# Linear attention ahead of a mixture of experts: row-tiled projections, column-tiled sums, and gates moved to the expert steps

## The chip, the core and the metric

The kernel runs on one core of one Trainium2 chip. The metric is device time in microseconds (us) of one execution; before the change it was 753.89 us (median of 3 runs, 752.79 to 762.47). The engines that matter are TensorE (PE in the profile; its weight loads are listed apart as PEld), VectorE (DVE), ScalarE (ACT), GpSimd (POOL) and the sequencer that issues most transfers (SP).

## The reference

Eight sequences of 576 tokens go through attention with random features (8 heads of 64 values, 128 features); each token is then sent to one of 8 experts.

```python
def phi(x):
    proj = np.einsum('bhsd,md->bhsm', x, omega)
    h = proj - np.sum(x * x, axis=-1, keepdims=True) / 2.0
    h = h - np.max(h, axis=-1, keepdims=True)
    return np.exp(h) / np.sqrt(m)
q_p, k_p = phi(q * scale), phi(k * scale)
kv = np.einsum('bhsm,bhsd->bhmd', k_p, v)
z = np.sum(k_p, axis=2)
x = einsum(q_p, kv) / (einsum(q_p, z) + 1e-06)          # (4608, 512) after a transpose
...
logits = normalized(x) @ normalized(expert_emb).T / tau
expert_idx = np.argmax(logits, axis=1)
gate_w = softmax(logits) at expert_idx
out[token] = gate_w * (relu(x @ w1[e]) @ w2[e])          # 512 -> 1024 -> 512
```

Inputs and outputs are float32. The term with the square of x cancels in the subtraction of the maximum, so the kernel leaves it out.

## The kernel before

**Attention.** The tokens are 36 tiles of 128 rows (`NTILE`), nine tiles for a pair of sequences (`TPS`), so that the fifth tile of nine (u = 4) has 64 rows of each. A loop over i does the key side of tile i and, `LAG` = 6 iterations later, the query side of tile iq = i - 6. All work of an iteration comes in two halves of four heads each:

- `halves` (L303) splits the loaded keys or queries into a high and a low part on POOL (L309, L310), and `feats` (L313) makes the projection from three products of 256 columns for each pair of heads (L319: high by high, high by low, low by high). In such a product the transposed features of omega are laid out block-diagonally for two heads of 64 values, so all 128 rows of the array are used. DVE takes the maximum of each head (L324), ACT the exponential, one head at a time (L327).
- `kvmm` (L330) adds features times values (with a column of ones) into PSUM, one product for each head, 128 features wide and 65 columns long (L341); after a sequence `kvfin`, `kvfin1`, `kvfin2` (L351, L356, L366) copy the sums, turn them and multiply them with the expert embedding, so that the logits come out as eight more columns.
- `qtr` (L377) turns the query features with four transposes for a half (L381) and copies them out on ACT (L385) or DVE (L387).
- `num` (L391) multiplies them with the sums (L405; the numerator, the denominator and the logits, 73 columns for each head). In a tile with u = 4 the product is written in two parts of 64 tokens, each with its own sums. DVE then divides (L408 to L414), and ACT sums the squares of the tile (L420).
- Every three tiles (`G`) `route`, `route1` and `gates` find the expert of each token, its place, and its gate: the norm by `root` (a Newton iteration of small DVE operations, L119 to L130), the softmax by one small exponential (L444). POOL then scatters the rows of the three tiles with the gate and the token's number behind them to DRAM (L471).

PE and POOL follow the order in which the code is written (a manual schedule); a scheduler orders DVE and ACT. The transposes of `qtr` are written between the products of `kvmm`.

**Tail of attention.** Once the fullest expert is known (`pick_first`, after tile 17), its weights are loaded and split, and `first_steps` (here called the fill, in pieces of three products) computes two tiles of 128 of its tokens between the last iterations and in the planning that follows: DVE works out a table of 38 expert steps (L662 to L734), which PE turns (L738) and SP reads (`tabi`, L739).

**Expert steps.** From t = 2 on each step takes 128 tokens of one expert: 24 products of 512 columns for the first layer (`pa`) and 24 for the second (`po`), float32 in three products of split halves (L251). The turned activations go through transposing DMAs (L815), with ACT and DVE copies around them (L808, L809, L827, L829, L841 to L847). Each step also splits one quarter of the next expert's weights (L216, L217), multiplies the result by the gate (`scaled`, L258) and scatters it (L261). Here all engines follow the code.

## Time and profile before

| | |
|---|---|
| median of 3 runs | 753.89 us |
| profiled execution | 756.55 us, its span 754.9 us |
| six first tiles, keys only | to 33.8 us |
| 30 tiles, keys and queries | 33.8 to 266.4 us |
| last six query tiles, fill, planning | 266.4 to 335.0 us |
| expert steps | from 335.0 us on |
| PE, DVE, ACT, POOL busy | 96%, 73%, 51%, 55% |

The rows below that begin with two times are from the timeline: start and duration in us, engine, line, operation, output and inputs, the number of instructions that the row joins, and in brackets the idle time before it with what ended it. Durations overlap, since a following instruction begins while the one before it is finishing; what an instruction costs in a busy queue is therefore the distance between two starts. A row of the windows gives a stretch, its length, the busy time of PE, PEld, DVE, ACT and POOL with their instructions, then the granted TensorE clock, the share of the DMA engines and GB/s.

### The profile page before, as it was taken

The numbers are of one execution on the slowest core, as the hardware profiler recorded it, in microseconds if no ns is written. First come the engines' busy times: TensorE is split into PE (matmuls) and PEld (weight loads), VectorE is DVE, ScalarE is ACT, GpSimd is POOL, SyncE is SP. The second block draws the span as 40 slices with busy tenths as digits, with TensorE's granted clock in tenths as the row PEclk, the third lists the DMA queues.
The fourth block names the chain that finished last, engine by engine and source line by source line (L and its number), as shares of the span: only waits on it lengthen the run. The fifth ranks groups of instructions, "written<-read, shape, count | busy, mean of one in ns | idle before, by whom it ended". The sixth has DMA issues, their size and how long they took to land. (4 is left out here: it accounts for less than half of the span.)

```text
span 754.9 us, 15226 instructions
## 1 busy us (share of the span) xinstructions
PE 722.3 (96%) x4475; PEld 628.6 (83%) x4476; DVE 549.5 (73%) x1288; ACT 381.8 (51%) x974; POOL 416.7 (55%) x385
## 2 busy tenths in 40 slices
PE   6899999999998988989999999999999999999994
PEld 6899999999888978877788888888888888888883
DVE  6468888998899888836579766686676676676661
ACT  4577777776786765425224334434434334434320
POOL 5754665677648843244456546456546546545544
PEclk9899999999999999999999999999999999999998
DMA  6543344454584421179587877977877887887730
GB/s 200 154 142 87 114 154 142 127 169 144 160 273 123 160 70 58 57 245 289 149 224 221 233 189 210 233 189 213 228 188 209 224 199 211 220 210 202 199 106 38
DMA packets 142353, 131.38 MB, mean 174 GB/s; under 512 B 106745, under 2 KB 106873, under 8 KB 142275
## 3 DMA queue, kind: packets, MB, share of 16 engines
q1 hardware_dynamic: 135954, 110.15, 53.2%
q0 software_dynamic: 6320, 20.23, 7.0%
q8 instruction: 43, 0.70, 0.4%
q14 instruction: 36, 0.29, 0.1%
HBM read 83.65 MB, written 21.80 MB: 140 GB/s over the span
## 5 line engine op out<-in xcount | busy, mean ns | idle before, releaser
L217 POOL TENSOR_TENSOR w1l<-raww,w1h 128x1024 f32 x34 | 89.0, 2616 | 158.0 <-DVE w1h L216 158.0
L251 PE MATMUL po<-w2h,hl 128*128 (+1 forms) x288 | 114.3, 397 | 0.2 <-DVE hl L847 0.2
L251 PE MATMUL po<-w2h,hh 128*128 (+1 forms) x288 | 114.4, 397 | 0.0
L251 PE MATMUL po<-w2l,hh 128*128 (+1 forms) x288 | 114.2, 396 | 0.0
L808 ACT ACTIVATE pl<-pa 128x512 uint16<-128x512 uint16 x68 | 40.4, 596 | 141.2 <-PE pa L251 130.9
L251 PE MATMUL pa<-w1h,xh 128*128 (+1 forms) x280 | 111.4, 398 | 0.0
L251 PE MATMUL pa<-w1l,xh 128*128 (+1 forms) x280 | 111.0, 396 | 0.0
L251 PE MATMUL pa<-w1h,xl 128*128 (+1 forms) x280 | 111.0, 396 | 0.0
L327 ACT ACTIVATE ftk<-pjk,nmk 128x128 f32<-128x128 f32 x288 | 82.8, 376 | 52.9 <-DVE nmk L324 27.9
L809 DVE COPY pl<-pa 128x512 uint16<-128x512 uint16 x68 | 46.8, 690 | 68.4 <-ACT pl L808 68.3
L327 ACT ACTIVATE ftq<-pjq,nmq 128x128 f32<-128x128 f32 x288 | 84.5, 396 | 13.0 <-DVE nmq L324 7.6
L827 DVE COPY wd<-t 128x1024 uint16<-128x1024 uint16 x68 | 86.0, 1269 | 0.4 <-DMA t<-pl 0.4
L217 POOL TENSOR_TENSOR w2l<-raww,w2h 128x1024 f32 x34 | 82.2, 2418 | 6.7 <-DVE w2h L216 5.3
L341 PE MATMUL kva<-vt,ftk 128*128 128x65 f32 x576 | 85.4, 260 | 0.0
L341 PEld LDWEIGHTS kva<-vt,ftk 128*128 128x128 f32 x576 | 82.4, 197 | 0.0
L381 PE MATMUL tr<-ident,ftq 128*128 128x128 f32 x288 | 75.0, 281 | 1.9 <-ACT qp L385 1.7
L405 PE MATMUL pn<-kvs,qp 128*128 128x73 f32 (+1 forms) x640 | 71.7, 264 | 3.1 <-DVE xr L414 3.1
L843 ACT ACTIVATE hh<-wd 128x1024 fp32r<-128x1024 f32 x34 | 36.1, 1061 | 72.0 <-DVE wd L827 72.0
L405 PEld LDWEIGHTS pn<-kvs,qp 128*128 128x128 f32 (+1 forms) x640 | 67.7, 182 | 5.0 <-DVE xr L414 2.3
L319 PE MATMUL pjk<-w1l,w1h 128*128 128x256 f32 x288 | 63.2, 312 | 5.5 <-DVE w1h L309 5.5
L251 PEld LDWEIGHTS po<-w2h,hl 128*128 128x128 f32 x288 | 54.2, 188 | 13.8 <-DVE hl L847 0.7
L251 PEld LDWEIGHTS po<-w2h,hh 128*128 128x128 f32 x288 | 54.3, 188 | 13.3 <-POOL w2l L217 0.3
(237 smaller groups left out, 1610.9 us busy)
## 6 DMA issues: line engine op xcount, KB each, us to landing
raww<-w1q SPq DMA_DIRECT2D x38, 512.0 KB
raww<-w2q SPq DMA_DIRECT2D x38, 512.0 KB
vt<-v SPq DMA_DIRECT2D x36, 260.0 KB
kt<-kT SPq DMA_DIRECT2D x36, 256.0 KB
qt<-qT SPq DMA_DIRECT2D x36, 256.0 KB
xgp<-xs SPq DMA_DIRECT2D x20, 257.0 KB
xg<-xs SPq DMA_DIRECT2D x18, 257.0 KB
rf<-w1q SPq DMA_DIRECT2D x4, 512.0 KB
```

The source lines that it names most:

```text
L217: il = nc.gpsimd.tensor_tensor(at(l, dp), raw, at(h, dp).bitcast(F32), op=ALU.subtract)
L251: done.append(nc.tensor.matmul(dst, x[:, c * P : (c + 1) * P], ws.rearrange("p o f -> p (o f)"), start=(begin and i == 0 and k == 0), stop ...
L319: nc.tensor.matmul(pj[:, 2 * a : 2 * a + 2, :].rearrange("p a m -> p (a m)"), x[:, 2 * half + a, :], o, start=n == 0, stop=n == 2,)
L327: nc.scalar.activation(ft[:, h, :], pj[:, h, :], AF.Exp, bias=nm[:, h : h + 1])
L341: nc.tensor.matmul(acc[:, h, :], ft[:, h, :], vt[:, 4 * half + h, :], start=begin and h == 0, stop=u == 4 + 4 * b and h == 3,)
L381: nc.tensor.transpose(tr[:, h * P : (h + 1) * P], ft[:, h, :], ident)
L405: nc.tensor.matmul(pn[lo:hi, h, :], qp[:, h, lo:hi], kvs[sb, b][:, 4 * half + h, :], start=True, stop=True)
L808: nc.scalar.activation(planes[1][:, o : o + 512], halved(src)[:, :, 1], AF.Copy)
L809: nc.vector.tensor_copy(planes[0][:, o : o + 512], halved(src)[:, :, 0])
L827: nc.vector.tensor_copy(to, src)
L843: nc.scalar.activation(hh, wd[:, 0:F], AF.Relu)
```

## The change

In attention the loads of 64 values for a head stay in plain float32, with no split. A half is now made of the heads of one parity: `a` = 0 has its values in rows 0 to 63 of the array and `a` = 1 in rows 64 to 127, and `proj` writes the products of two such halves (one of the keys, one of the queries) alternately, into different banks. `kvmm`, `num` and the logits of the sums write each product in two parts of 64 output rows. The outputs of `num` for the two parities are two fixed tiles `nu[0]` and `nu[1]`; the transposes of a = 0 and the turns of the sums use them too, while the last query transposes (when no keys are left) take banks of their own. The whole loop is written out for DVE and ACT as well. `root` may run on POOL and does so for the embedding. The norm and the softmax leave attention: the row in DRAM carries the eight shifted logits in place of the gate, and the expert steps sum the squares, take a root, and make the gates for three steps at once. The fill runs in two to four pieces an iteration.

```diff
-PAY = DM + 2
+PAY = DM + E + 1
...
+    nu = [ps.tile([P, 512], F32, name=f"nu{a}") for a in range(2)]
...
+    def squares(xg, n2, junk):
+        nc.scalar.activation(junk, xg[:, 0:DM], AF.Square, accum_out=n2)
...
+    def exps(xg, nrm, total):
...
+        nc.scalar.activation(junk, xg[:, DM : DM + E], AF.Exp, scale=nrm, accum_out=total)
...
-            halves("k", i, kt)
...
+        def proj(*which):
+            for w, i, a, tag in which:
+                st["pj" + w, i, a] = ps.tile([P, 4, M], F32, name=f"pj{w}{i}_{a}", tag=tag, bufs=2)
+            for c in range(4):
+                for w, i, a, _ in which:
+                    r = slice(a * D, (a + 1) * D)
+                    nc.tensor.matmul(st["pj" + w, i, a][:, c, :], st[w, i][r, c, :], om[r, :], start=True, stop=True)
...
-                nc.tensor.matmul(
-                    acc[:, h, :], ft[:, h, :], vt[:, 4 * half + h, :],
...
+                for c in range(0, P, 64):
+                    nc.tensor.matmul(
+                        acc[c : c + 64, h, :], ft[:, h, c : c + 64], vt[:, 2 * h + a, :],
...
+        def qtr(i, a, own):
+            tr = nu[1] if a == 0 and not own else ps.tile([P, 512], F32, name=f"tr{i}_{a}", tag="py", bufs=2)
...
+        pn = [b[:, 0 : 4 * (D + 1 + E)].rearrange("p (h w) -> p h w", h=4) for b in nu]
+        def num(i):
...
+            parts = [(u > 4, 0, D), (u >= 4, D, P)]
...
-            if half == 1:
-                sq = small.tile([P, DM], BF16, name=f"sq{i}", tag="sq", bufs=1)
-                nc.scalar.activation(sq, st["xr", i][:, 0:DM], AF.Square, accum_out=st["n2", g][:, gi : gi + 1])
...
-        def gates(g):
...
-            nrm = root(small, n2, G, f"g{g}")
...
+        loop.enter_context(tc.manual_schedule(engines={ET.DVE, ET.Activation}))
         for i in range(NTILE + LAG + 1):
...
+            if ks and qs:
+                pairs = [("k", i, 0, "py"), ("q", iq, 1, "py")], [("k", i, 1, "px"), ("q", iq, 0, "px")]
...
+            proj(*pairs[0])
+            proj(*pairs[1])
+            if later is not None:
+                num_out(later)
...
+                    kvmm(i - 1, a, b or int(u > 4))
...
+                for a in (1, 0) if late else (0, 1):
+                    qtr(iq - 1, a, not ks)
+                qcopy(iq - 1, 1, True)
...
+            if qs and iq >= 2:
+                num(iq - 2)
...
+        def roots_of(b):
+            rough[b] = few("rough", f"b{b}", 3)
+            nc.scalar.activation(rough[b], n2s[b], AF.Sqrt, bias=tiny)
...
+        def norms_of(b):
...
+            nc.vector.reciprocal(nrms[b], rough[b])
...
+            if t == SHIFT - 1 or t > SHIFT and t % 3 == 0:
+                roots_of(batch(t)[0])
+            elif t == SHIFT or t > SHIFT and t % 3 == 1:
+                norms_of(batch(t)[0] if t > SHIFT else 0)
+                exps_of(batch(t)[0] if t > SHIFT else 0)
+            elif t > SHIFT:
+                inverted(totals[batch(t)[0] - 1])
...
+            elif NPRE + 2 < t < NSTAT - 2:
+                squares_of(t + 2)
```

TensorE at iteration 13 before, its second half: `pjk13` and `pjq7` are the projections of the keys of tile 13 and the queries of tile 7, `kva` the sums, `tr6` the transposes, `pn6` the numerators.

```order
L319 MATMUL pjk13_1_1364<-w1l_109 128x256
L319 MATMUL pjq7_1_1378<-w1l_109,w2h_110 128x256 x2
L319 MATMUL pjq7_1_1378<-w1l_109,w2l_111 128x256
L319 MATMUL pjq7_1_1378<-w1l_109,w2h_110 128x256 x2
L319 MATMUL pjq7_1_1378<-w1l_109,w2l_111 128x256
L341 MATMUL kva1_0_1_974<-vt12_878,ftk12_1_1253 128x65
L381 MATMUL tr6_1_1393<-ident_70,ftq6_1_1267 128x128
```

TensorE at the same iteration after the change, from the last pair of its projections to the first of the next iteration:

```order
L321 MATMUL pjk13_1_1232<-om_131,kt13_960 128x128
L321 MATMUL pjq7_0_1233<-om_131,qt7_966 128x128
L345 MATMUL kva1_0_0_893<-vt12v_845,ftk12_0_1130 64x65 x8
L345 MATMUL kva1_0_1_902<-vt12v_845,ftk12_1_1178 64x65 x8
L391 MATMUL nu1_71<-ident_72,ftq6_0_1187 128x128 x4
L391 MATMUL tr6_1_1286<-ident_72,ftq6_1_1137 128x128 x4
L410 MATMUL nu0_70<-kvs0_1_787,qp5_0_1183 64x73 x8
L410 MATMUL nu1_71<-kvs0_1_787,qp5_1_1174 64x73 x8
L321 MATMUL pjk14_0_1336<-om_131,kt14_1091 128x128
```

The halves are gone: both projections of an iteration stand first, the transposes no longer stand between the sums, and the numerators are those of a tile one further back (5 beside the transposes of 6).

DVE before, around the maxima of iteration 14 (`rr`, `lg`, `xr`: the division; `rtt_g`, `rt_g`: the root of the gates):

```order
L324 TENSOR_REDUCE nmq8_0_1448<-pjq8_0_1441 128x4
L410 TENSOR_TENSOR lg2_1403<-pn6_0_1405,rr6_0_1412 128x32
L414 TENSOR_TENSOR xr6_1401<-pn6_0_1405,rr6_0_1412 128x256
L119 TENSOR_SCALAR rtt_g1_1522<-n21_994 128x3
L408 TENSOR_SCALAR rr6_1_1473<-pn6_1_1466 128x4
L121 TENSOR_SCALAR rt_g1_1521<-rtt_g1_1522 128x3
L409 RECIPROCAL rr6_1_1473<-rr6_1_1473 128x4
L124 TENSOR_TENSOR rtt_g1_1522<-n21_994,rt_g1_1521 128x3
```

DVE after, from the end of iteration 15 on: the copy out of the transposes of `nu[1]`, the last maximum, the rest of a routing, and the division of tile 7.

```order
L399 COPY qp8_0_1576<-nu1_71 128x512
L327 TENSOR_REDUCE nmq9_0_1578<-pjq9_0_1495 128x4
L463 TENSOR_TENSOR base1_1553<-base1_1553,sel1_126 128x24
L465 TENSOR_REDUCE pos1_1602<-base1_1553 128x3
L473 CAST posi01_1604<-pos1_1602 128x1
L423 TENSOR_SCALAR rr7_1637<-nu0_70 128x4
L423 TENSOR_SCALAR rr7_1637<-nu1_71 128x4
L424 RECIPROCAL rr7_1637<-rr7_1637 128x8
L426 TENSOR_TENSOR lg2_1506<-nu0_70,rr7_1637 128x32
L430 TENSOR_TENSOR xr7_1635<-nu0_70,rr7_1637 128x4x64
L426 TENSOR_TENSOR lg2_1506<-nu1_71,rr7_1637 128x32
L430 TENSOR_TENSOR xr7_1635<-nu1_71,rr7_1637 128x4x64
```

The root is gone from DVE's queue here; one reciprocal serves both parities, and the division comes in one piece, behind the copy of `nu[1]` and ahead of the next iteration's maxima.

ACT in an expert step before: `hh14` is the last operation of one step, `pl16` the first of the next (the outputs of the first layer, taken apart for the transposing DMA).

```order
L841 ACTIVATE xh16_6871<-wd14_6860 128x512
L843 ACTIVATE hh14_6874<-wd14_6860 128x1024
L808 ACTIVATE pl16_1_6984<-pa16_0_7018 128x512
L808 ACTIVATE pl16_1_6984<-xgp0_105 128x512
L829 ACTIVATE wd15_7048<-t16_15_0_6866 128x512
```

ACT at the same place after (`sq` the squares, `ex` the exponentials of the gates of steps 14 to 16):

```order
L898 ACTIVATE xh16_6681<-wd14_6670 128x512
L900 ACTIVATE hh14_6684<-wd14_6670 128x1024
L253 ACTIVATE sq17_6714,n2b5_6713<-xg5_5178 128x512
L262 ACT_TABLE_LOAD
L262 ACTIVATE ex_14_6728,totalb4_6727<-xgp2_107,nrmb4_6721 128x8
L262 ACTIVATE ex_15_6730,totalb4_6727<-xg3_5176,nrmb4_6721 128x8
L262 ACTIVATE ex_16_6732,totalb4_6727<-xg4_5177,nrmb4_6721 128x8
L865 ACTIVATE pl16_1_6809<-pa16_0_6843 128x512
```

Between `hh14` and `pl16` now stand the squares, a load of another function table and three exponentials; a step earlier it is the squares, a table load and one square root.

More of the change, by code (lines that the diff above doesn't have):

```diff
@@ L313, in feats @@
[L313 to L323 removed]
+                st["q", i] = p1.tile([P, 4, P], F32, name=f"qt{i}", tag="qt", bufs=2)
@@ L380, in qtr @@
             for h in range(4):
[L381 to L391 removed]
+                nc.tensor.transpose(tr[:, h * P : (h + 1) * P], st["fq", i, a][:, h, :], ident)
@@ L402, in num @@
-            parts = [(0, 0, P)] if u < 4 else [(1, 0, P)] if u > 4 else [(0, 0, D), (1, D, P)]
-            for h in range(4):
-                for b, lo, hi in parts:
-                    nc.tensor.matmul(pn[lo:hi, h, :], qp[:, h, lo:hi], kvs[sb, b][:, 4 * half + h, :], start=True, stop=True)
-                next(between, None)
-            rr = small.tile([P, 4], F32, name=f"rr{i}_{half}", tag="rr", bufs=3)
-            nc.vector.tensor_scalar(rr, pn[:, :, D], EPS, None, op0=ALU.add)
-            nc.vector.reciprocal(rr, rr)
@@ L536, in first_steps @@
                 turned(xgp[t], 0, new(f"x{t}", f"kv{t}"), *pre_x[t])
+                squares(xgp[t], n2[:, t : t + 1], hs[t][:, 0:DM])
                 yield
+            nrm = root(gp, n2, NPRE, "p", nc.gpsimd)
             yield from up(0, 0, range(4), new("a00", "kv0"))
+            norms(nrm)
             yield from up(0, 1, range(4), new("a01", "kv1"))
+            for t in range(NPRE):
+                exps(xgp[t], nrm[:, t : t + 1], total[:, t : t + 1])
             pa = new("a10", "kv0")
@@ L544, in first_steps @@
             yield from turn(0, 1, "kv1")
-            yield from up(1, 1, range(4), new("a11", "pj"))
+            inverted(total)
+            yield from up(1, 1, range(4), new("a11", "px"))
             po = new("o0", "kv0")
@@ L597, in emb2, with go, filled @@
             nc.vector.tensor_copy(enbd[D:P, :, 1, :], ev[D:P])
-        after = {}
-        todo, later, fill = {(1, 1): [(emb1,)], (3, 1): [(emb2,)]}, None, first_steps()
+        spare, mid, ends = {}, {}, {}
+        at = lambda d, *key: d.setdefault(key, [])
+        for i, f in ((1, emb0), (3, emb1), (4, emb2)):
+            at(ends, i).append((f,))
+        later, fill = None, first_steps()
+        def go(d, *key):
+            for f, *a in d.pop(key, ()):
+                f(*a)
+        def filled(n):
+            for _ in range(n):
+                next(fill, None)
@@ new lines, in attention_moe @@
+            late = bool(spare.get((i,)))
+            go(spare, i)
+            if later is not None and later % G == G - 1 and later < NTILE - 1:
+                steps = routed(later // G)
+                for d, key in ((mid, i), (ends, i), (spare, i + 1), (mid, i + 1), (ends, i + 1), (ends, i + 2), (ends, i + 3)):
+                    key = min(key, NTILE + LAG)
+                    at(d, key).append((next, steps, None))
+            go(mid, i)
+            if not qs and iq >= 2:
+                num(iq - 2)
@@ new lines, in attention_moe @@
+            if iq >= 1:
+                for a in (1, 0) if late else (0, 1):
+                    qtr(iq - 1, a, not ks)
+                qcopy(iq - 1, 1, True)
+            if 0 <= i - 1 < NTILE and u == 4 and i >= LAG:
+                for a in range(2):
+                    kvmm(i - 1, a, 1)
+            for p in pairs[1][:1]:
+                feats(*p[:3])
+            if iq >= 1:
+                qcopy(iq - 1, 0, False)
+            for p in pairs[1][1:]:
+                feats(*p[:3])
+            if filling:
+                filled(1 if i <= NTILE + 2 else 2)
@@ new lines, in attention_moe @@
+            if qs and iq >= 2:
+                num(iq - 2)
+            go(ends, i)
+            if filling:
+                filled(1)
+            n = iq - 3 * GPICK - 6
+            if 1 <= n < 2 * NQ + 1:
+                at(ends, i + 1).append((first_split, n - 1))
+            if 0 <= n < 2 * NQ:
+                first_weights(n)
+        loop.close()
+        assert not any(d for d in (spare, mid, ends)), (spare, mid, ends)
+        num_out(NTILE - 2)
+        num(NTILE - 1)
+        num_out(NTILE - 1)
@@ L654, in attention_moe @@
+        steps = routed(NTILE // G - 1)
+        next(steps)
+        next(steps)
         for _ in range(FILL1):
             next(fill, None)
-        route1(NTILE // G - 1)
+        for _ in steps:
+            pass
         vt = nc.vector
```

460 lines of the change are left out of this document (228 added, 232 removed).

## The prediction

> **What bounds the kernel now.** I read the windows by stage first, then the timeline of TensorE and DVE in one tile, then the expert steps.
>
> ```profile
> 0.00:20.00 20.00, 12.84 (x90) 12.05 (x91) 12.38 (x39) 8.73 (x28) 10.62 (x26) 1.00 0.61 199
> 60.00:260.00 200.00, 193.77 (x1817) 189.45 (x1817) 173.90 (x598) 148.64 (x503) 127.63 (x170) 1.00 0.48 154
> 343.00:740.00 397.00, 396.76 (x1709) 318.84 (x1708) 279.83 (x342) 156.64 (x235) 214.28 (x105) 1.00 0.76 203
> ```
>
> In the middle of attention PE is busy for 97% of the time and DVE for 87%, at the full clock; in the expert steps PE is busy all the time and DVE for 70%. Both stages are PE's, but in attention DVE is close behind: what PE gives up there is a gain only down to what DVE needs.
>
> ```profile
> 33.81 0.40 PE L319 MATMUL pjq<-w1l,w2h 128*128 128x256 f32 x2
> ...
> 150.37 0.33 PE L341 MATMUL kva<-vt,ftk 128*128 128x65 f32 x2
> 150.54 0.28 PE L381 MATMUL tr<-ident,ftq 128*128 128x128 f32 x1
> 150.66 1.01 PE L405 MATMUL pn<-kvs,qp 128*128 128x73 f32 x8
> 151.47 0.48 PE L319 MATMUL pjk<-w1l,w1h 128*128 128x256 f32 x2
> ...
> 152.27 0.40 PE L319 MATMUL pjq<-w1l,w2h 128*128 128x256 f32 x2
> ...
> 152.63 0.40 PE L319 MATMUL pjq<-w1l,w2h 128*128 128x256 f32 x2
> ...
> 154.94 0.48 PE L319 MATMUL pjk<-w1l,w1h 128*128 128x256 f32 x2
> ...
> 266.37 0.48 PE L319 MATMUL pjq<-w1l,w2h 128*128 128x256 f32 x2
> ```
>
> The first query projection starts at 33.81 us and that of tile 30 at 266.37: 232.6 us for 30 tiles, 7.75 us each. An undisturbed half takes 154.94 - 151.47 = 3.47 us of PE, a tile 6.94. Its parts, by distance of starts: three projection products 0.36 (152.27 to 152.63), so 0.12 for one and 24 × 0.12 = 2.9 us a tile; a sum (two instructions, since a plain float32 product is two) 0.17 and a transpose 0.12, together 8 × 0.29 = 2.3 us; eight numerator instructions 0.81, so 1.6 us a tile. Every ninth tile adds eight sums, and twice in nine tiles the sums are turned and multiplied with the embedding (four transposes, four products): at the same prices (1.6 + 1.0 + 1.6) / 9 = 0.5 us a tile. PE thus needs 7.4 of the 7.75 us.
>
> **The change in attention, PE.** The numerators of a mixed tile (u = 4) already have the new form of 64 output rows:
>
> ```profile
> 74.22 0.28 PE L381 MATMUL tr<-ident,ftq 128*128 128x128 f32 x1
> 74.43 0.73 PE L405 MATMUL pn<-kvs,qp 128*64 128x73 f32 x16
> 75.09 0.50 PE L319 MATMUL pjk<-w1l,w1h 128*128 128x256 f32 x2
> ```
>
> Sixteen instructions take 75.09 - 74.43 = 0.66 us where eight of the wide form took 0.81, so two column tiles do run beside each other, at 0.08 us a pair. The price holds the way out of the form; the way in is the start of the first one 0.21 us after the transpose instead of 0.12, 0.09 more.
>
> By a rule of the Trainium skill ("TensorE: Matmul & The Clock Gate", section "Part 3: Packing small matmuls — row/col tiling") a weight load overlaps with running matmuls only where the row group differs, which speaks against column tiles. By that rule 16 column-tiled pairs would cost no less than 16 wide instructions, 1.6 us and not 1.3 for the numerators and as much for the sums, some 0.6 us a tile more than I count. The 0.66 us against 0.81 above contradict it.
>
> Per tile, after: numerators 2 × 0.66 = 1.3 us; sums in the same form at the same price 1.3 (65 columns, so rather less); eight transposes 1.0; two entries into column form, at 0.09, 0.2. The projections are 16 float32 products, 32 instructions, in pairs on the upper and lower 64 rows. No row shows row tiles. Each instruction streams 128 columns in two passes, as long as the 256 of a product at 0.12. If the two row groups run beside each other, 16 × 0.12 = 1.9 us; at the price of the column pairs it would be 16 × 0.08 = 1.3; if they run one after the other, 32 × 0.12 = 3.8. I take 1.9, the length of the row that streams as much, halved because the column pairs show that halves of the array do overlap. Sum 5.7, with the ninth-tile extras at the new prices ((1.3 + 1.0 + 1.3) / 9 = 0.4) 6.1 us: 1.3 us under the 7.4 before. The shorter sums and transposes standing in a row may take off 0.2 to 0.4.
>
> **The change in attention, DVE and ACT.**
>
> ```profile
> 132.53 0.16 DVE L408 TENSOR_SCALAR rr<-pn 128x4 f32<-128x4 f32 x1 [0.98 <-PE pn L405]
> ...
> 132.94 0.19 DVE L410 TENSOR_TENSOR lg<-pn,rr 128x32 f32<-128x32 f32 x1
> 133.05 0.41 DVE L414 TENSOR_TENSOR xr<-pn,rr 128x256 f32<-128x256 f32 x1
> 133.38 0.51 DVE L426 TENSOR_REDUCE raw<-lg 128x24 f32<-128x192 f32 x1
> 133.80 0.68 DVE L324 TENSOR_REDUCE nmk<-pjk 128x4 f32<-128x512 f32 x1
> 134.40 0.17 DVE L428 TENSOR_REDUCE mx<-raw 128x3 f32<-128x24 f32 x1
> ...
> 135.71 0.68 DVE L387 COPY qp<-tr 128x512 f32<-128x512 f32 x1
> 136.31 0.17 DVE L431 SCALAR_TENSOR_TENSOR sel<-raw,iotm 128x24 bf16<-128x24 f32 x1
> ```
>
> A maximum costs 0.60 us (133.80 to 134.40), a copy 0.60 (135.71 to 136.31), two small operations that depend on each other about 0.2 apiece (132.53 to 132.94 for two). A tile keeps four maxima 2.4, a copy 0.6, and a division of 0.1 + 0.41 + 2 × (0.11 + 0.33) = 1.4. Routing without its root is 0.42 and some ten small ones at 0.1 to 0.2, about 2.2 for three tiles, 0.7; turning the sums is two copies and a small one, 1.4 twice in nine tiles, 0.3. Sum 5.4 us. Gone are the root and softmax, some 20 small operations for three tiles (0.7 to 1.3 us a tile at those prices). POOL loses the splits; its scatters, three together before, now stand one in an iteration, and only the six buffers of rows wait for them.
>
> ```profile
> 0.97 1.28 ACT L327 ACT_TABLE_LOAD   x1 [0.97 <-PEq L1012]
> ...
> 103.12 0.63 ACT L420 ACTIVATE sq<-xr 128x512 bf16<-128x512 f32 x1 [0.16 <-DVE gt L447]
> ...
> 103.75 1.12 ACT L327 ACTIVATE ftk<-pjk,nmk 128x128 f32<-128x128 f32 x4
> 104.75 1.16 ACT L327 ACTIVATE ftq<-pjq,nmq 128x128 f32<-128x128 f32 x4
> ```
>
> ACT keeps 16 exponentials, 1.00 us for four, 4.0, and a copy of about 0.6; the squares (103.12 to 103.75, 0.6) leave: 4.8 with the copies of the sums.
>
> The new order adds one loop through three engines. The last maximum of an iteration stands behind DVE's copy of `nu[1]`, and the next iteration's second pair of projections waits for the exponentials behind that maximum: copy 0.6, maximum 0.7, exponentials 1.1, then on PE that pair 1.0, the sums 1.3 and four transposes 0.5, and a tail of 0.2 (a transpose lasts 0.28, the next starts after 0.12): 5.4 us. What is queued behind the waiting projection is all the rest of PE's iteration; behind DVE's wait for the transposes stand the last maximum and the division. PE 6.1 less a bit, DVE 5.4, the loop 5.4, ACT 4.8. I take 6.0 us a tile; the bounds are 5.6 (PE with the cheaper sums and no idle) and 6.6 (the same slack above the largest sum that DVE has now, 7.75 to 7.0). **Gain: 30 × (7.75 - 6.0) = 52.5 us.**
>
> **The start.** The six key-only tiles take to 33.8 us. The seven key, six value and one query transfers that precede the first query projection are 14 × 0.26 = 3.6 MB, at the 199 GB/s of the first 20 us 18 us, so with the first 2 us 20 us at the least. Now they are asked for four tiles ahead, no split stands between them and PE, and the embedding's root is on POOL. PE has 1.0 + 1.3 us a tile, DVE 1.2, ACT 2.0, so the transfers set the pace. I take 22.5 us, bounds 20 and 28: **gain 11 us**.
>
> **The tail.**
>
> ```profile
> 310.41 1.01 PE L405 MATMUL pn<-kvs,qp 128*128 128x73 f32 x8
> ...
> 335.01 0.39 PE L251 MATMUL pa<-w1h 128*128 128x512 f32 x1
> ...
> 353.94 0.40 PE L251 MATMUL pa<-w1h,xh 128*128 x1
> ```
>
> From 266.4 to the end of the last numerator at 311.2 are 44.8 us. PE's queries-only iterations are 1.0 + 1.0 + 1.3 + 0.2 = 3.5 us, two with two pieces of fill (0.70 each, three products at the 0.234 us of the expert steps below), four with four: with the first, which still has keys' sums, 6 + 2 × 4.9 + 3 × 6.3 + 5 = 39.7, gain 5. Twenty fill pieces are done by then instead of ten, and the rows are scattered without waiting for a gate, so the first product at 335.0 can come 7 us (ten pieces) sooner; but the planning does not shorten as much, and the fifth step, at 353.9, needs weights that are only asked for after it. I take 5 of the 7, bounds 0 and 8. **Gain 10 us**.
>
> **The expert steps.**
>
> ```profile
> 437.79 0.68 DVE L846 TENSOR_TENSOR xl<-wd,xh 128x512 fp32r<-128x512 f32 x1
> ...
> 440.50 0.39 PE L251 MATMUL pa<-w1h,xh 128*128 x1
> ...
> 443.56 0.60 ACT L808 ACTIVATE pl<-pa 128x512 uint16<-128x512 uint16 x1 [4.56 <-PE pa L251]
> 444.19 0.69 DVE L809 COPY pl<-pa 128x512 uint16<-128x512 uint16 x1 [1.54 <-ACT pl L808]
> ...
> 451.75 0.39 PE L251 MATMUL pa<-w1h,xh 128*128 x1
> ```
>
> A step is 451.75 - 440.50 = 11.25 us of 48 products without a gap. ACT gains 0.6 us of squares in each, and in three steps two table loads at 1.28, a root and three short exponentials, at no more than 0.4 each since four of 128 columns take 1.12: at most 0.6 + 1.3 + 1.2 = 3.1 us in one step, ahead of the `pl` before which it now idles 4.56 us. DVE gains some 1.2 us of small operations in a step, in front of an idle time of 1.54. The next step's `xl` is ready at 438.5, 2.0 us before its product. I count nothing; if the cover were gone, 12 × 6.0 us (0.6 × 3 + 2 × 1.28 + 4 × 0.4) = 72.
>
> **Sum.** 754.9 - 52.5 - 11 - 10 = 681.4, with the 1.65 us outside the span 683.0; the profiled run lies 2.7 us over the median, so about **680 us**.
>
> **The rivals.**
>
> 1. *Row tiles don't overlap.* The projections cost 3.8 us, PE 8.0 a tile: 7.75 × 8.0 / 7.4 = 8.4 us at the worst; the cheaper sums and weight-load-bound pairs of 0.10 bring it to 7.5. With starts and tail nearly as above, 725 to 755, say 740. For it: no row shows it. Against: column tiles overlap.
>
> 2. *Each change of the array's form drains it.* Four changes a tile; the column form costs 0.09 to enter, but the row form isn't in the trace and could cost a matmul's whole length (0.28 us). That is 4 × 0.28 - 0.2 = 0.9 us a tile, 30 × 0.9 = 27 us: 707. The Trainium skill ("TensorEngine Tiling (Array Packing)", section "Key Properties") says that a change of tiling mode drains TensorE; this trace agrees, with 0.09 us for one kind of change.
>
> 3. *The clock falls, and it gets slower.*
>
> ```profile
> 17.17 1.00 PE L341 MATMUL kva<-vt,ftk 128*128 128x65 f32 x8
> ...
> 21.29 0.41 PE L594 MATMUL eps__340<-ident,embq 8*128 8x8 f32 x4 [2.35 <-DVE embq L589]
> ...
> 23.97 1.80 PE L341 MATMUL kva<-vt,ftk 128*128 128x65 f32 x8
> ```
>
> After PE idled for 2.35 us the same eight instructions took 1.80 us instead of 1.00. If half-used arrays and PE's waits in each iteration cost the clock through attention, PE's 6.1 us become 6.1 × 1.8 = 11, the 30 tiles 98 us longer instead of 52 shorter, the total near 830. It decides from a factor of 7.75 / 6.1 = 1.27 on. Against: no wait that I count on exceeds 1 us, and PE stays busy over 90%.
>
> 4. *DVE or ACT become the bound of the expert steps* (the cover above fails): 680 + 72 = 752 at the worst, no change; half of it 716.
>
> **How the numbers follow.** Forecast 0.78 (own range 662 to 702: 5.6 to 6.5 us a tile, and the other bounds), rival 1 0.08, rival 2 0.07, rival 3 0.03, rival 4 0.04. A measurement of this kernel tells about 2% (15 us) from no change. Faster by over 2%: the forecast, rival 2, half of 1 and of 4, 0.91; slower: rival 3, 0.03; the rest, 0.06, the same. The range from 660 to 720 holds the forecast and rival 2 and half of 4.
>
> **What would show it.** First query projection at 20 to 25 us; 5.6 to 6.5 us between tiles; a run of 16 projection instructions in about 1.0 us (2.0 if rival 1 holds); the `nu` numerators 0.6 to 0.7 us for 16; DVE busy near 90% in attention, with its waits on PE's transposes; the clock at 1.00; 11.25 us an expert step, with ACT's idle time before `pl` down to 1 to 4 us. Tiles over 7 us, a clock under 0.9 in attention, or steps over 11.5 us would make it wrong.

## The result, and the profile after

The changed kernel takes 716.09 us (median of 4 runs, 714.29 to 717.29) against 753.34 us for the kernel before in the same comparison: a ratio of 0.9513, with a 95% interval of 0.9478 to 0.9547. The profiled execution took 715.48 us, its span 713.9 us. So 41.0 us of span went, where the prediction had 73.5.

The first view is the starts of three products on PE, from the timeline of the changed kernel; the prediction has the same three of before, at 33.81, 266.37 and 353.94 us. (`pjq` is the first query projection of a tile, `pa` the first product of the fifth step. The two tiles of the fill count as the first two steps, 0 and 1, so the expert steps begin with t = 2 and the fifth step is t = 4.)

```profile
24.73 0.37 PE L321 MATMUL pjq<-om,qt 64*128 64x128 f32 x1 [0.41 <-ACT ftk L330]
...
221.72 0.48 PE L321 MATMUL pjq<-om,qt 64*128 64x128 f32 x2
...
312.48 0.40 PE L242 MATMUL pa<-w1h,xh 128*128 x1
```

| stretch | before, us | after, us | gained | predicted |
|---|---|---|---|---|
| to the first query projection | 33.81 | 24.73 | 9.1 | 11 |
| 30 tiles | 232.56 (7.75 each) | 196.99 (6.57 each) | 35.6 | 52.5 |
| from there to the fifth step | 87.57 | 90.76 | -3.2 | 10 |
| from there to the end of the span | 400.96 | 401.42 | -0.5 | 0 |

The windows of the changed kernel that answer to the middle of attention and to the expert steps of before; the last row is the stretch from the first product of step t = 2 to that of t = 4:

```profile
60.00:220.00 160.00, 150.88 (x2807) 134.60 (x2807) 135.81 (x429) 124.39 (x430) 47.58 (x97) 1.00 0.58 193
320.00:690.00 370.00, 369.40 (x1592) 296.96 (x1591) 337.34 (x406) 208.57 (x391) 200.30 (x100) 1.00 0.79 204
...
288.50:312.50 24.00, 20.87 (x89) 16.21 (x90) 10.51 (x11) 11.83 (x18) 10.10 (x8) 0.93 0.84 277
```

In attention PE is busy for 94% of the time, DVE for 85% and ACT for 78%, at the full clock. In the expert steps PE has no gap, as before (369.40 of 370 us), although DVE is now busy for 91% and ACT for 56%.

One tile of the changed kernel, from its timeline (an iteration begins with its first projections, at 155.21 us, and the next at 160.75):

```profile
155.21 0.37 PE L321 MATMUL pjk<-om,kt 64*128 64x128 f32 x1
155.22 0.37 PE L321 MATMUL pjq<-om,qt 64*128 64x128 f32 x1
157.47 1.15 PE L345 MATMUL kva<-vt25v,ftk 128*64 128x65 f32 x32
158.55 0.66 PE L391 MATMUL nu<-ident,ftq 128*128 128x128 f32 x4
...
159.57 1.25 PE L410 MATMUL nu<-kvs,qp 128*64 128x73 f32 x32
160.75 0.37 PE L321 MATMUL pjk<-om,kt 64*128 64x128 f32 x1
```

By distance of starts this is 2.26 us for the projections, 1.08 for the sums, 1.02 for eight transposes and 1.18 for the numerators, together 5.54 us. None of the 30 tiles is shorter, and four are as short as this one; the mean is 6.57. These four have no routing, no turn of the sums, no logits product and no second block of sums on PE. Iterations with one of these take 6.2 to 8.2 us from the third tile on, although that work by itself is 0.1 to 1.0 us; four more without it take 6.0 to 7.1. The rest of this section shows what they wait for, at an earlier tile, where the routing's four small products stand between sums and transposes:

```profile
123.21 1.14 ACT L330 ACTIVATE ftq<-pjq,nmq 128x128 f32<-128x128 f32 x4
123.23 0.37 PE L321 MATMUL pjk<-om,kt 64*128 64x128 f32 x1
...
123.45 0.27 PE L321 MATMUL pjk<-om,kt 64*128 64x128 f32 x1
...
123.56 0.27 PE L321 MATMUL pjk<-om,kt 64*128 64x128 f32 x1
...
124.41 0.37 PE L321 MATMUL pjq<-om,qt 64*128 64x128 f32 x1
...
125.49 1.15 PE L345 MATMUL kva<-vt20v,ftk 128*64 128x65 f32 x32
...
128.00 1.59 PE L410 MATMUL nu<-kvs,qp 128*64 128x73 f32 x32
128.11 0.69 DVE L399 COPY qp<-nu 128x512 f32<-128x512 f32 x1 [0.26 <-PE nu L391]
...
128.85 0.58 PEld L410 LDWEIGHTS nu<-kvs,qp 128*64 128x64 f32 x16 [0.27 <-DVE qp L399]
```

Two hand-overs show. The exponentials of the last query half end at 123.21 + 1.14 = 124.35 us, and the second pair's query products, which write into the bank that these have read, start at 124.41; the projections of this tile take 125.49 - 123.23 = 2.26 us, against 1.99 in the tile at 142.06 us, where nothing is waited for:

```profile
142.06 0.37 PE L321 MATMUL pjk<-om,kt 64*128 64x128 f32 x1
...
144.05 0.34 PE L345 MATMUL kva<-vt23v,ftk 128*64 128x65 f32 x4
```

And the second parity's numerators stand still until DVE has copied the transposes out of `nu[1]`: 128.85 - 128.00 = 0.85 us for the first sixteen instructions, of which 0.66 is work. Added up over the 30 tiles (by distance of starts of each block, and against the shortest block of its kind): projections 75.2 us, of which 59.7 at the shortest, 1.99 each; sums 35.6; transposes 31.3; numerators 41.7, of which 33.9 at the shortest 1.13; the turns of the sums, their products with the embedding and the routing 13.2. The shortest forms of all blocks make 5.12 us a tile and 0.37 of extras in the mean, 5.49; the other 1.08 us are taken as waits (some 0.1 of it is the sums, which mostly take 1.08 us and not their shortest 0.98; no row shows a wait there).

### The profile page after: what moved, and what is told of

It is laid out like the page before. It is cut to its first block, busy times and chain, and to the rows that moved or that the text cites. A ratio compares the mean times of both kernels' runs of the same rounds, so it can differ in the third digit from the quotient of the medians.

```text
span 713.9 us, 17995 instructions
## 1 busy us (share of the span) xinstructions
PE 668.1 (94%) x5977; PEld 554.5 (78%) x5978; DVE 570.5 (80%) x1134; ACT 419.9 (59%) x1074; POOL 301.8 (42%) x296
## 5 line engine op out<-in xcount | busy, mean ns | idle before, releaser
L242 PE MATMUL nu<-w2h,hh 128*128 (+1 forms) x288 | 114.0, 396 | 0.7 <-POOL w2l L208 0.7
L242 PE MATMUL nu<-w2h,hl 128*128 (+1 forms) x288 | 113.8, 395 | 0.0
L242 PE MATMUL nu<-w2l,hh 128*128 (+1 forms) x288 | 113.7, 395 | 0.0
L321 PE MATMUL pjk<-om,kt 64*128 64x128 f32 x576 | 75.6, 293 | 6.6 <-DMA kt<-kT 5.2
L321 PE MATMUL pjq<-om,qt 64*128 64x128 f32 x576 | 76.5, 286 | 4.9 <-ACT ftq L330 3.6
L321 PEld LDWEIGHTS pjk<-om,kt 64*128 64x128 f32 x576 | 66.2, 197 | 9.5 <-DVE om L574 4.9
L321 PEld LDWEIGHTS pjq<-om,qt 64*128 64x128 f32 x576 | 64.4, 189 | 8.5 <-ACT ftq L330 4.9
L242 PEld LDWEIGHTS nu<-w2h,hh 128*128 128x128 f32 x288 | 54.2, 188 | 14.1 <-POOL w2l L208 1.4
L242 PEld LDWEIGHTS nu<-w2h,hl 128*128 128x128 f32 x288 | 54.2, 188 | 13.1 <-DVE hl L904 0.4
L242 PEld LDWEIGHTS nu<-w2l,hh 128*128 128x128 f32 x288 | 54.2, 188 | 12.7
```

What stands on the lines that cost most here:

```text
L242: done.append(nc.tensor.matmul(dst, x[:, c * P : (c + 1) * P], ws.rearrange("p o f -> p (o f)"), start=(begin and i == 0 and k == 0), stop ...
L321: nc.tensor.matmul(st["pj" + w, i, a][:, c, :], st[w, i][r, c, :], om[r, :], start=True, stop=True)
```

## The experiments

### What the new forms of the products cost

**Rows in turn.** The two products of a pair are written one after the other instead of alternately:

```diff
-            for c in range(4):
-                for w, i, a, _ in which:
+            for w, i, a, _ in which:
+                for c in range(4):
```

> The changed kernel with one edit: the two products of a pair of projections are no longer written in turn by row half, but all four heads of one half and then all four of the other. The same 32 instructions of 64 rows. Theory (two row halves run beside each other only when neighbours in the queue belong to different halves): the projections of a tile go from 2.25 us to about 32 x 0.11 = 3.6 us, the tile from 6.57 to about 7.9 us, the total from 716 to about 755 us. Rival (the loop of copy, maximum, exponentials and second pair sets the tile, PE has room): the tile stays under 6.9 us and the total under 726 us.

It took 737.63 us, 21.5 us more than the changed kernel; 7.09 us a tile, and the first query projection started at 31.01 us instead of 24.73. Neither number was met: the projections went to 3.09 us, not to 3.6. The timeline of one tile's projections shows why. In the queue stand eight instructions of `pjk`, eight of `pjq`, and the same again:

```profile
150.01 0.82 PE L321 MATMUL pjk<-om,kt 64*128 64x128 f32 x5
150.57 0.37 PE L321 MATMUL pjq<-om,qt 64*128 64x128 f32 x1
150.67 0.27 PE L321 MATMUL pjk<-om,kt 64*128 64x128 f32 x1
...
151.00 0.72 PE L321 MATMUL pjq<-om,qt 64*128 64x128 f32 x5
```

The first `pjq` starts 0.01 us after the fifth `pjk` and before the three `pjk` that stand ahead of it. The same order stands in 27 of the 29 tiles that were counted. So here TensorE ran two row halves beside each other when they were no more than some four instructions apart, and out of the order of the queue. Alternating them is worth 1.1 us of PE a tile, of which 7.09 - 6.57 = 0.52 us reached the total: the rest took the place of waits.

**Whole columns.** The sums and the numerators go back to products of 128 output rows; only the mixed tile keeps its two parts.

```diff
-                for c in range(0, P, 64):
-                    nc.tensor.matmul(
-                        acc[c : c + 64, h, :], ft[:, h, c : c + 64], vt[:, 2 * h + a, :],
+                nc.tensor.matmul(
+                    acc[:, h, :], ft[:, h, :], vt[:, 2 * h + a, :],
...
-            parts = [(u > 4, 0, D), (u >= 4, D, P)]
+            parts = [(u > 4, 0, D), (u >= 4, D, P)] if u == 4 else [(u > 4, 0, P)]
```

> The changed kernel with the sums and the numerators back in products of 128 output rows (only the mixed tile keeps its two parts); projections, transposes, order and banks stay. Theory (PE's own work sets the tile): the sums go from 1.08 to 8 x 0.17 = 1.4 us, the numerators from 1.18 to 1.6 us, the tile from 6.57 to 7.2 to 7.4 us, the total to about 738 us. Rival (the loop through DVE and ACT sets the tile): less than 0.3 us a tile, total under 725 us.

It took 747.43 us, 31.3 us more and 9 us past the theory; 7.44 us a tile, a little past what the theory had. The timeline of a mixed tile (two blocks of sums):

```profile
155.29 2.00 PE L344 MATMUL kva<-vt22v,ftk 128*128 128x65 f32 x16
157.12 0.61 PE L390 MATMUL nu<-ident,ftq 128*128 128x128 f32 x4
...
158.00 1.90 PE L344 MATMUL kva<-vt22v,ftk 128*128 128x65 f32 x16
```

Sixteen wide instructions take 157.12 - 155.29 = 1.83 us in a row, 0.115 each, where 32 column-tiled ones took 1.08. A pair of column tiles thus takes 1.08 / 16 = 0.07 us, the way into the form included, where one wide instruction takes 0.115. That is 0.75 us a tile less for the sums, and about as much for the numerators. I had priced the wide form from before, where a sum and a transpose stood alternately (0.17 us for the two instructions of a sum), and it is dearer in a row of its own. The rule of the Trainium skill ("TensorE: Matmul & The Clock Gate", section "Part 3: Packing small matmuls — row/col tiling") that a weight load overlaps with running matmuls only where the row group differs does not hold for these column tiles: they share their rows, and without an overlap a pair could not be shorter than the one wide instruction, 0.07 us against 0.115.

The two edits add 1.1 and 1.5 us of PE to a tile, and the tile grows by 0.52 and 0.87 us. Of the 1.08 us of waits about 0.6 are therefore slack that more PE work fills, and PE sets the rest of the time. Both halves of the change, rows and columns, are needed for the gain: without the columns' part it is nearly gone (747.43 us against 757.58 for the kernel before in the same comparison, a ratio of 0.987 with an interval of 0.975 to 0.999). No run puts the norm and the softmax back into attention, so what their move gave is not shown.

### Separate banks

The two banks of the numerators become one tile of two banks, in place of two tiles:

```diff
-    nu = [ps.tile([P, 512], F32, name=f"nu{a}") for a in range(2)]
+    nus = ps.tile([P, 2, 512], F32, name="nus")
+    nu = [nus[:, a] for a in range(2)]
```

> The changed kernel with the two numerator banks made as one tile of two banks instead of two tiles; nothing else. The numerators of the first parity then wait on TensorE for the copy that only the other parity's bank needs. Theory (that copy is on the path): the 0.66 us of the first eight numerators no longer run beside the copy, 0.5 to 0.7 us a tile, total 731 to 737 us. Rival (the wait falls where TensorE would wait later anyway): total under 722 us.

It took 735.84 us, inside what the theory had, but mostly for another reason. The group of the numerators on PE between 60 and 220 us, of the changed kernel and then of this one (the last column is PE's idle time ahead of the group and what ended it); then, from the end of this one, DVE's scaling of the last but one step and the first product of PE that waited:

```profile
L410 PE MATMUL nu<-kvs,qp 128*64 128x73 f32 x779 | 33.9, 231 | 3.7 <-DVE qp L399 2.3
```

```profile
L411 PE MATMUL nus<-kvs,qp 128*64 128x73 f32 x738 | 28.8, 229 | 15.6 <-DVE qp L400 15.5
...
706.61 0.75 DVE L250 TENSOR_SCALAR xg<-nus,totalb 128x512 f32<-128x512 f32 x1 [4.50 <-PE nus L243]
...
711.26 0.80 PE L243 MATMUL nus<-w2h,hh 128*128 x1 [4.69 <-POOL w2l L209]
```

The wait for the copy grew by 12 us in 160, as expected, but the tile only went from 6.57 to 6.79 us, since the projections then waited less for the exponentials (67.5 us in 30 tiles instead of 75.2). Attention lost 7.4 us, and 10.9 of the 20.0 us of span were lost after the last step's first product: there the same banks take the second layer's results, and the last step's products of the second layer waited 4.69 us (0.28 in the changed kernel) where the profile names POOL. Behind that stands the shared tile again. DVE's scaling of the step before, which reads one bank, starts only at 706.61 us, after 4.50 us of waiting for PE, which writes the other; in the changed kernel it starts at 693.09 us, while PE is still writing. The last split of weights stands behind it on DVE and POOL. The products after the wait take 0.43 us instead of 0.23 until 716 us, at a granted clock of 0.50, some 2.4 us in all, and the last scatter starts 5.2 us after the start of the last product instead of 1.9. The theory was right on the wait, but had only a part of the places where it falls.

### The fill's pacing

The fill gets two pieces in each of the last five iterations, ten in place of twenty:

```diff
-            filling = i > NTILE
+            filling = i >= NTILE + 2
...
-                filled(1 if i <= NTILE + 2 else 2)
-            if filling:
-                filled(1 if i > NTILE + 2 else 0)
+                filled(1)
```

> The changed kernel with the pacing of the fill as it was: two pieces in each of the last five iterations, ten in all instead of twenty; the other ten stand behind the table of expert steps again. Theory (twenty early pieces lengthen the last iterations and leave TensorE nothing to do while the first rows and weights arrive): the last numerator ends 4 to 7 us earlier, the stretch from the first to the third step goes from 24.0 back to about 19 us, the total from 716 to 705 to 710 us. Rival (the last iterations are bound by DVE and the planning by its own chain): within 2 us of 716 us.

It took 705.77 us, in the middle of the theory's range. The changed kernel's timeline around its first expert steps:

```profile
288.50 0.50 PE L242 MATMUL pa<-w1h 128*128 128x512 f32 x1 [0.69 <-ACT w1h L229]
...
293.84 0.63 PE L228 MATMUL pt<-ident,xg 128*128 128x128 f32 x4 [2.05 <-DMA xg<-xs]
...
294.68 0.63 PE L242 MATMUL pa<-w1l,w1h 128*128 128x512 f32 x1
295.11 1.06 PE L242 MATMUL pa<-w1h 128*128 128x512 f32 x2
...
299.89 1.14 PE L228 MATMUL ph<-ident,wd 128*128 128x128 f32 x8 [1.08 <-ACT wd L998]
```

All 38 pieces are done when the table is turned, and PE has nothing to do while the first rows are fetched: 2.05 us of waiting, after which the products take 0.43 us instead of 0.23 for four microseconds, and 1.08 us more. The same places with ten pieces left over:

```profile
283.67 0.39 PE L242 MATMUL pa<-w1h 128*128 128x512 f32 x1
...
286.40 0.60 PE L228 MATMUL pt<-ident,xg 128*128 128x128 f32 x4
...
290.36 1.15 PE L228 MATMUL ph<-ident,wd 128*128 128x128 f32 x8 [0.61 <-ACT wd L996]
...
302.97 0.40 PE L242 MATMUL pa<-w1h,xh 128*128 x1
```

From the first product of step t = 2 to that of t = 4 it is now 302.97 - 283.67 = 19.3 us instead of 312.48 - 288.50 = 24.0, and the last numerators end 8.4 us earlier (the next product at 262.71 against 271.15 us). From the 30th tile to the fifth step it is 84.0 us against 90.8, so 6.7 of the 9.7 us of span come from the pacing; the other 3 us are from the first two query tiles, which this edit does not touch. The windows of these two tiles, of the changed kernel and of this one (the third number from the end is the granted clock):

```profile
24.73:38.57 13.84, 12.09 (x154) 10.85 (x154) 5.19 (x9) 7.01 (x26) 0.00 (x0) 0.75 0.44 135
```

```profile
24.82:35.83 11.01, 9.26 (x155) 8.14 (x155) 5.19 (x9) 6.76 (x25) 0.00 (x0) 1.00 0.47 143
```

They took 13.84 us at a clock of 0.75 there and 11.01 us at 1.00 here. The other 28 tiles take 6.54 us each in both kernels, so the 6.47 us a tile of this one, over all 30, is no gain of the edit. Below I therefore give the mean of these 28 tiles beside that of the 30. This kernel is the base of the next seven.

### Which loop holds a tile

I had named one loop: copy of `nu[1]`, last maximum, exponentials, second pair of projections. Four edits move one operation each.

**The maximum ahead of the copy, and the copy on ACT:**

```diff
-            if iq >= 1:
-                qcopy(iq - 1, 0, False)
             for p in pairs[1][1:]:
                 feats(*p[:3])
+            if iq >= 1:
+                qcopy(iq - 1, 0, False)
```

> On the kernel of fill_ten (705.8 us, 6.47 us a tile over its first 30): DVE does the last maximum of an iteration ahead of its copy of nu[1] instead of behind it. The prediction's loop (copy, maximum, exponentials, second pair) would shorten by the 0.6 us of the maximum: 6.1 us a tile or less, total about 695 us. Theory now (the loop that binds runs from the division through the first maximum and then through sixteen exponentials and a copy that stand on ACT without a gap; the last exponentials wait for ACT and not for the maximum): the tile stays within 0.15 us of what it was, total 703 to 710 us.

```diff
                 qcopy(iq - 1, 1, True)
+                qcopy(iq - 1, 0, True)
...
-            if iq >= 1:
-                qcopy(iq - 1, 0, False)
```

> On the kernel of fill_ten: the copy of nu[1] is done by ACT, right behind its copy of the other parity, instead of by DVE. DVE loses 0.6 us a tile, ACT gains 0.5 us ahead of the last exponentials. If DVE and the loop through its copy bind: 6.1 us a tile or less, total about 695 us. Theory now (ACT's unbroken run from the first to the last exponential is part of the loop): 0.2 to 0.5 us a tile more, total 711 to 720 us.

They took 708.31 and 708.87 us, with 6.58 and 6.65 us a tile, over the 30 and over the 28 alike (the base has 6.47 and 6.54). Both speak against the prediction's loop, which should have become 0.6 us shorter. The first met the number of the second theory; the second lost less than that theory had (711 to 720). The groups of PE with the maximum ahead of the copy:

```profile
L321 PE MATMUL pjq<-om,qt 64*128 64x128 f32 x397 | 52.2, 280 | 1.1 <-ACT ftq L330 1.1
...
L410 PE MATMUL nu<-kvs,qp 128*64 128x73 f32 x768 | 33.8, 232 | 12.8 <-DVE qp L399 6.6 <-DVE posi L473 6.1
```

The projections became shorter (68.5 us in 30 tiles instead of 74.6), and the numerators waited instead, 52.2 us instead of 41.7: the copy now stands behind the maximum. The wait had only changed its place.

**The first maximum ahead of the division, and amid it:**

```diff
+            for p in pairs[0][:1]:
+                feats(*p[:3])
             if later is not None:
                 num_out(later)
-            for p in pairs[0][: 1 if i < LAG else 2]:
+            for p in pairs[0][1 : 1 if i < LAG else 2]:
                 feats(*p[:3])
```

> On the kernel of fill_ten: DVE does the first maximum of an iteration (keys, first parity) ahead of the division of the tile before instead of behind it. The first exponential can start 0.5 to 0.6 us earlier. Theory now (that start binds ACT's run and through it the second pair of projections): the projections go from 2.4 to about 2.0 us a tile, the tile from 6.47 to 6.0 to 6.2 us, total 692 to 700 us. Rival (the numerators' banks come free 0.6 us later with the later division, and the transposes into nu[1] and the turns of the sums wait for that): no gain, 705 to 712 us.

In the other, `num_out` stops after the division of the first parity:

```diff
-            if later is not None:
-                num_out(later)
-            for p in pairs[0][: 1 if i < LAG else 2]:
+            parts = num_out(later) if later is not None else iter(())
+            next(parts, None)
+            for p in pairs[0][:1]:
+                feats(*p[:3])
+            for _ in parts:
+                pass
+            for p in pairs[0][1 : 1 if i < LAG else 2]:
                 feats(*p[:3])
```

> On the kernel of fill_ten: the first maximum stands between the division of the first parity and that of the second. The first exponential starts 0.3 to 0.5 us earlier, and only nu[1] comes free later, by 0.6 us. Theory now: 6.1 to 6.3 us a tile, total 695 to 702 us. Rival (the later free nu[1] costs as much): 705 to 712 us.

They took 717.71 and 706.92 us, with 6.75 and 6.53 us a tile (6.74 and 6.49 over the 28). The theory of that moment fell as well: ACT's first exponentials no longer waited as long, but its second ones did, since their maximum now stood behind the division. ACT's groups between 60 and 220 us, on the base and then with the maximum first:

```profile
L330 ACT ACTIVATE ftq<-pjq,nmq 128x128 f32<-128x128 f32 x198 | 57.7, 396 | 0.7
L330 ACT ACTIVATE ftk<-pjk,nmk 128x128 f32<-128x128 f32 x196 | 57.0, 393 | 33.5 <-DVE nmk L327 33.2
```

```profile
L330 ACT ACTIVATE ftq<-pjq,nmq 128x128 f32<-128x128 f32 x192 | 55.5, 387 | 20.0 <-DVE nmq L327 16.9 <-DVE base L460 2.5
L330 ACT ACTIVATE ftk<-pjk,nmk 128x128 f32<-128x128 f32 x190 | 54.7, 382 | 17.9 <-DVE nmk L327 17.4
```

No order of DVE's operations that I tried shortens the tile by more than 0.05 us, which suggests that no single loop holds it, but DVE's operations as a whole, each waited for by one of the others. The next three take operations away instead of moving them.

### Taking work from DVE and ACT

The maximum of a query's features is a factor of its numerator and of its denominator and falls out in the division, but for the 1e-6. The first edit takes no maximum:

```diff
+            if which == "q":
+                for h in range(4):
+                    nc.scalar.activation(ft[:, h, :], pj[:, h, :], AF.Exp)
+                return
```

> On the kernel of fill_ten: the query features are exponentials without their maximum taken off (it cancels in the division of numerator by denominator; the sizes of these inputs allow it). DVE loses two maxima of 0.6 us a tile, ACT keeps its 16 exponentials. If DVE's place in the hand-overs (the numerators that wait for its copy, the last exponentials that wait for its maximum) is what costs: 5.8 to 6.1 us a tile instead of 6.47, total 691 to 697 us. If ACT's run of exponentials is: 6.3 us or more, 702 us or more.

The second takes one maximum of the row, and one exponential, for the four heads of a half:

```diff
+            if which == "q":
+                nc.vector.tensor_reduce(nm, flat(pj), axis=AX.X, op=ALU.max, negate=True)
+                nc.scalar.activation(flat(ft), flat(pj), AF.Exp, bias=nm)
+                return
```

> On the kernel of fill_ten: the four query heads of a half share one maximum of the row (it cancels in the same way), so that one exponential of 512 columns, about 0.55 us, takes the place of four, 1.0 us. ACT loses 0.9 us a tile, DVE keeps four maxima. If ACT's run of exponentials is what costs: the second pair of projections no longer waits (2.0 us a tile instead of 2.5), 5.9 to 6.1 us a tile, total 692 to 698 us. If DVE's place is: 6.3 us or more, 702 us or more.

The third has one exponential and no maximum:

```diff
+            if which == "q":
+                nc.scalar.activation(flat(ft), flat(pj), AF.Exp)
+                return
```

> On the kernel of fill_ten: both edits, no query maximum and one query exponential for four heads. DVE loses 1.2 us and ACT 0.9 us a tile. Theory (TensorE's own instructions come to about 5.5 us a tile, and all the rest of the 6.47 are waits at hand-overs with DVE and ACT): 5.5 to 5.7 us a tile, total 677 to 685 us. If something that no reading showed holds the tile (TensorE's price, transfers): 6.0 us or more, 692 us or more.

The three side by side, with the base. DVE and ACT are their busy shares from 60 to 200 us, times the mean of the 28 tiles, so busy us in one tile:

| kernel | DVE | ACT | 30 tiles | 28 tiles | total, us |
|---|---|---|---|---|---|
| base (`fill_ten`) | 5.56 | 5.12 | 6.47 | 6.54 | 705.77 |
| one exponential for four heads (`q_one_exp`) | 5.51 | 4.24 | 6.37 | 6.39 | 697.80 |
| no query maximum (`q_no_max`) | 4.40 | 4.39 | 6.13 | 6.19 | 691.67 |
| both (`q_neither`) | 4.40 | 4.01 | 6.08 | 6.14 | 690.68 |

`q_no_max` does not take work from DVE alone. Four of its query exponentials, which no longer take a maximum as bias, last 0.79 us from first to last, where four with one lasted 1.14 (at 123.21 us above):

```profile
112.19 0.79 ACT L330 ACTIVATE ftq<-pjq 128x128 f32<-128x128 f32 x4
```

So ACT loses 0.7 us a tile there as well. But `q_one_exp`, which takes 0.9 us from ACT and next to nothing from DVE, gains only 0.15 us over the 28 tiles, and taking DVE's 1.1 us away besides (`q_neither`, with another 0.2 less on ACT) gains 0.25 more. DVE's work thus weighs more than ACT's, though no run lightens DVE alone. With both, the tile came to 6.08 and not to the 5.5 to 5.7 that I expected. The windows and groups of the last one:

```profile
60.00:200.00 140.00, 134.08 (x2604) 120.81 (x2600) 100.45 (x355) 91.44 (x264) 43.51 (x85) 1.00 0.63 207
```

```profile
L321 PE MATMUL pjq<-om,qt 64*128 64x128 f32 x432 | 53.9, 281 | 0.7 <-ACT ftk L335 0.5 <-DMA qt<-qT 0.2
...
L415 PE MATMUL nu<-kvs,qp 128*64 128x73 f32 x846 | 36.2, 231 | 4.2 <-DVE posi L478 1.8 <-DVE qp L404 1.3
```

DVE is busy for 72% and ACT for 65%; the projections are down to 2.16 us a tile (64.7 in 30). The numerators have not moved: 42.6 us in 30 tiles, 0.3 us a tile over the shortest, because in the iterations with a turn, a logits product or a routing the transposes into `nu[1]` are written last and their copy cannot begin sooner. That remainder was not tried.

Of the 18.2 us of span between the base and the last kernel (704.2 and 686.0 us) attention's 30 tiles give 11.8, and the stretch from there to the first expert step 7.1. In that stretch the granted clock was 0.95 in the base and 1.00 in the last kernel; how much of the 7.1 us is the clock and how much the waits was not separated. The totals of the base and of the last three come from different comparisons: their ratios to the kernel before are 0.933 (interval 0.924 to 0.942) for the base and 0.920, 0.927 and 0.919 for the three, each give or take 0.006 or 0.007. These intervals meet that of the base, so the reading rests on the tiles. `q_one_exp` keeps a maximum of the row, so that its exponentials cannot overflow, whatever the size of the inputs.

## Why the prediction was right or wrong

The direction and the wide range were right, and the time lies at the range's upper end; the forecast of 680 us was 36 us too low, and the time lies outside its own 662 to 702. That it lies inside the wide one is luck as far as the mechanism goes: the range reached so high for rival 2 and for half of rival 4, and neither took place. Of the 36 us 32.5 are in the stages; for the rest, the forecast took off 2.7 us because the profiled run of before was above its median, and that of the changed kernel is 0.6 below. Point by point:

- **The middle of attention: the step that failed is "I take 6.0 us a tile", which set the tile by the largest of PE's sum, DVE's sum and one loop.** It measured 6.57, 17 us of the miss. PE's own terms were too high: 5.49 us instead of 6.1. Row tiles ran at 1.99 us for a tile's projections (1.9 taken), column-tiled sums at 0.98 to 1.08 and numerators at 1.13 to 1.18 (1.4 taken for each, with the entry into the form). For the row tiles the number was right, but its reason is not borne out: it took the time from the length that is streamed, and the wide instructions of `whole_columns`, which stream 65 columns and not 128, are 0.115 us apart as well. DVE's sum was near (5.4 taken, 85% of 6.57 = 5.6 measured). What was missing is the waits, 1.08 us a tile, for which the sum had nothing; only the upper bound of 6.6 allowed for them. With three engines at 78 to 94% that hand banks to each other several times in an iteration, the largest sum is a lower bound. The waits gather in the iterations with a routing, a turn, a logits product or second sums (6.2 to 8.2 us, against 5.54 for half of those without). The experiments that take DVE's and ACT's work away move the tile to 6.08, those that reorder it do not.
- **The loop of 5.4 us** was no bound of its own: its last maximum could be moved without a gain.
- **The tail: the step "gain 5 (iterations)" and "I take 5 of the 7" failed with its sign.** It lost 3.2 us where 10 were counted, 13 us of the miss. Ten more early pieces were not ten pieces of time won. They stood in the last iterations, and the same ten had covered the wait for the first rows of the expert steps. With the former pacing the stretch takes 84.0 us, a gain of 3.5 on before: half of the miss in the tail is the pacing, and for the other half the iterations and the planning got shorter by less than I had taken.
- **The start** came to 24.73 us (22.5 predicted, 20 to 25 in the list of signs).
- **The expert steps** were right. A step is 432.52 - 421.32 = 11.20 us, and ACT, with the squares in it, still idles 1.75 us before `pl` (1 to 4 predicted):

```profile
421.32 0.39 PE L242 MATMUL pa<-w1h,xh 128*128 x1
...
421.91 0.61 ACT L253 ACTIVATE sq<-xg 128x512 bf16<-128x512 f32 x1
...
424.37 0.60 ACT L865 ACTIVATE pl<-pa 128x512 uint16<-128x512 uint16 x1 [1.75 <-PE pa L242]
...
432.52 0.39 PE L242 MATMUL pa<-w1h,xh 128*128 x1
```

- **Rival 1** (row tiles don't overlap) is wrong: two instructions of a pair start 0.01 us apart and the next pair 0.11 later. **Rival 2** (each change of form drains 0.28 us): the first product of a pair is followed after 123.45 - 123.23 = 0.22 us, the next after 0.11, so entering the row form costs 0.1 us. Its time, 707, lies nearest to the measured one, but not by its mechanism. **Rival 3**: the granted clock is 1.00 from 60 to 220 us; in the first two query tiles it was 0.75, which cost 2.8 us by the comparison with `fill_ten`. **Rival 4**: its half price, 716 us, is the measured time by accident; the steps are as long as before.

## What to carry to other kernels

Where three engines are each busy for more than three quarters of a loop and pass PSUM banks around, add a term for hand-overs to the largest sum (here 1.0 us of 6.6), above all for the iterations with irregular extra work, and look for operations to take away rather than to reorder. Two halves of TensorE's array nearly halved the time of narrow products here, with the instructions of the two standing alternately in the queue. When two kernels are compared by a stage, look at the granted clock of that stage first: here 3 us of a difference in attention were the clock of two tiles. Work that fills an engine's wait is worth its time only at that wait: done earlier it lengthens what it stands in, and the wait can come back with a slower clock behind it.

## What was not expected of the hardware

TensorE started products of one row half ahead of products of the other half that stood before them in its queue, but only from some four instructions away (the first of eight beside the fifth of the eight ahead of it). The Trainium skill ("TensorE: Matmul & The Clock Gate", section "Part 3: Packing small matmuls — row/col tiling") calls matmuls strictly in order and names a window of 64 for pulling weight loads ahead; the rows at 150.57 and 150.67 us show neither the order nor so long a reach. Nor is it settled here how long a wait costs the clock. In the changed kernel PE's wait of 2.05 us before 293.84 us was followed by 4 us at a granted clock of 0.57 (the row below), but one of 2.34 us before 236.90 us was not followed by any loss (1.00 until 255 us):

```profile
294.20:298.20 4.00, 4.00 (x14) 3.17 (x13) 0.00 (x0) 0.40 (x1) 0.61 (x1) 0.57 0.93 313
```
